# A long convolution with an MLP behind it: second DFT stage on half-height tiles, real and imaginary part on the two halves of the partitions, kv made channel-major

## The chip, the cores and the metric

One core of a Trainium2 chip. The time is the device time of one launch in microseconds (us). Engines are named as in the profile: PE is TensorE (PEld its weight loads), DVE is VectorE, ACT is ScalarE, POOL is GpSimd, SP is SyncE, which here only issues DMAs. PEclk is the TensorE clock that was granted, as a share of full speed.

## The reference

S = 2048 tokens, D = 512 channels, hidden width 1376, all inputs bf16. Part A is a gated long convolution, part B an MLP; both stand on a layer norm of what comes in, and both are added to it:

```python
def _A_ref(q, k, v, shift_k, ssm_k, ssm_D):          # q is layernorm(x)
    k_shift = zeros_like(k)                           # a causal filter of 4 taps per channel
    for t in range(ks):
        k_shift = k_shift + k_pad[:, t:t + S, :] * shift_k[:, ks - 1 - t][None, None, :]
    kv = k_shift * v
    kv_f = rfft(pad(kv, 2 * S)); kf_f = rfft(pad(ssm_k, 2 * S))     # per channel, over time, f32
    y = irfft(kv_f * kf_f)[:S] + kv * ssm_D[None, None, :]
    return q * y
h  = x + _A_ref(layernorm(x), k, v, shift_k, ssm_k, ssm_D)
h2 = h + relu(layernorm(h) @ w1) @ w2                # 512 -> 1376 -> 512
```

## The kernel before

The convolution is done per channel by a DFT of two stages with time split as t = 64 n1 + n2 (n1 below 32, n2 below 64) and frequency as 32 k1 by 64 k2. A channel is written d = 128 rg + 64 dp + g: rg picks one of four row groups, dp a half, g one of 64.

- **Loading (lines 155 to 248).** SP issues k and v in 4 KB rows per partition (`_load_p16`, 32 partitions per DMA; `kh`, `vt`), the filter `ssm_k` in one DMA (`sk`, 2 MB), and `ssm_D`, broadcast to `dtab_b`. PE transposes `sk` (L229), ACT copies the results into `kfl` (L230), whose partitions are (rg, n1). DFT tables are computed on chip: POOL makes indices, DVE phases (`_phase`), ACT sines (`_sin`, `_cos`). `cc`, `cs`, `cn` are [128, 32, 128] in float32r and block-diagonal: 64 x 64 blocks for dp = 0 and 1, zeros elsewhere.
- **Taps (L251 to L263).** DVE makes kv with tokens on the partitions: 8 chunks of 8 operations on 128 x 1024 elements. PE and ACT re-lay it into `xfl` (L277, L283).
- **Stage 1 (`_stage1`, L99 and L101), for the filter and then for kv:** 512 matmuls of 32 rows by 64 columns in four row groups, the table as a bf16 sum of two parts. 32 evacuations of 128 x 512 (all on ACT for the filter, L270; alternating ACT and DVE for kv, L302 and L304) write `a1k` or `a1x`: partitions (dp, n2), then 64 values (real and imaginary of each k1) by 256 channels (rg, g).
- **Stage 2 (`_stage2`, L112 to L115):** per k1 four full matmuls of 256 columns give the real and the imaginary part, [128, 2, 256] in PSUM, partitions (dp, k2). For the filter DVE and ACT store them into `kf` (L292 adds `ssm_D`, L294). For kv they are multiplied by `kf` straight from PSUM: DVE takes 3/4 of the columns (L334, L335: 128 x 384 each), POOL the last quarter (L336, L337) after ACT has copied it to SBUF (L333). Three k1 later `finish` adds the products up on PE (L344 to L347, identity and minus identity), and ACT writes the result over `kf` (L348).
- **Inverse, first stage (L388 to L396):** for each g two accumulating matmuls with `kf` as the stationary side (its elements 512 bytes apart) and 256 table columns moving; ACT and DVE copy into `bp`. In program order the layer-norm statistics of x (L382, L383) come before it; x itself (`xh`) is loaded behind the products.
- **Inverse, second stage, and MLP (L413 to L486):** `inv2_group` does 256 f32 matmuls in 32 x 32 tiles, reading `bp` at steps of 1 KB, then gate, residual, layer norm and transposes for four token tiles; `mlp1` and `mlp2` are bf16 matmuls with 512 columns; the groups are interleaved by hand.

The tile framework places the waits and moves independent instructions of an engine past each other by its own estimate; on the chip each engine then runs its list in order, and so does SP with its DMAs.

Of the kernel before, what the change touches and what calls it, by code (L numbers as in the profile page):

```python
# [8 lines left out]
ACT = mybir.ActivationFunctionType  # L9
# [9 lines left out]

# [33 lines left out]
def _phase(nc, pool, r_i32, col, F, M, name):  # L53
    t = pool.tile([P, F], I32, name=f"{name}_ti")
    nc.vector.tensor_scalar(out=t[:], in0=r_i32, scalar1=col[:], scalar2=float(M // 2), op0=ALU.mult, op1=ALU.add)
    nc.vector.tensor_single_scalar(out=t[:], in_=t[:], scalar=M - 1, op=ALU.bitwise_and)
    ph = pool.tile([P, F], F32, name=f"{name}_ph")
    nc.vector.tensor_single_scalar(out=ph[:], in_=t[:], scalar=-(M // 2), op=ALU.add)
    aph = pool.tile([P, F], F32, name=f"{name}_aph")
    nc.vector.tensor_scalar(out=aph[:], in0=t[:], scalar1=-1.0, scalar2=float(M // 2), op0=ALU.mult, op1=ALU.add)  # L60
    nc.vector.tensor_tensor(out=aph[:], in0=aph[:], in1=ph[:], op=ALU.max)
    return ph, aph


def _sin(nc, out, ph, M, neg=False):
    scale = 2.0 * math.pi / M * SIN_SHRINK
    nc.scalar.activation(out=out, in_=ph, func=ACT.Sin, scale=(-scale if neg else scale))


def _cos(nc, out, aph, M, halfpi):  # L70
    scale = 2.0 * math.pi / M * SIN_SHRINK
    nc.scalar.activation(out=out, in_=aph, func=ACT.Sin, scale=-scale, bias=halfpi[:])


def _load_p16(nc, dst, src2d, eng, halo=0, rows=None):
    S, D = src2d.shape
    r0, r1 = rows if rows is not None else (0, 16 + halo)
    for a in range(4):
        if halo and a == 0 and r0 < halo:
            ap = bass.AP(tensor=src2d.tensor, offset=src2d.offset, ap=[[64 * D, 32], [D, r1 - halo], [1, D]])  # L80
            eng.dma_start(out=dst[0:32, halo:r1, :], in_=ap)
            nc.vector.memset(dst[0:1, 0:halo, :], 0.0)
            ah = bass.AP(tensor=src2d.tensor, offset=src2d.offset + (64 - halo) * D, ap=[[64 * D, 31], [D, halo], [1, D]])
            eng.dma_start(out=dst[1:32, 0:halo, :], in_=ah)
        else:
            ap = bass.AP(tensor=src2d.tensor, offset=src2d.offset + (16 * a - halo + r0) * D,
                         ap=[[64 * D, 32], [D, r1 - r0], [1, D]])
            eng.dma_start(out=dst[32 * a:32 * a + 32, r0:r1, :], in_=ap)


def _stage1(nc, psum, src_fl, f1hi, f1lo, a_out, evac):
    cnt = 0
    for gb in range(8):
        pss = [psum.tile([P, 8, 64], F32, tag="ps", name=f"ps1_{rg}") for rg in range(4)]
        for gi in range(8):
            g = 8 * gb + gi
            for rg in range(4):
                rows = slice(32 * rg, 32 * rg + 32)
                nc.tensor.matmul(out=pss[rg][:, gi, :], lhsT=src_fl[rows, g, :, :], rhs=f1hi[rows, :],  # L99
                                 start=True, stop=False, tile_position=(32 * rg, 0))  # L100
                nc.tensor.matmul(out=pss[rg][:, gi, :], lhsT=src_fl[rows, g, :, :], rhs=f1lo[rows, :],  # L101
                                 start=False, stop=True, tile_position=(32 * rg, 0))
        for rg in range(4):
            j0 = 64 * rg + 8 * gb
            evac(cnt, a_out[:, :, j0:j0 + 8], pss[rg][:].rearrange("p g c -> p c g"))
            cnt += 1
# [411 lines left out]
```

## Time and profile before

| what | us |
|---|---|
| three runs | 291.29, 290.19, 288.76; median 290.19 |
| span of the profiled execution (first to last instruction) | 287.4 |
| mean granted PE clock in it | 0.85 |

The page gives no other time for that execution. By stage, from the busy times in windows (us busy in the window):

| window | stage | PE | DVE | ACT | POOL | PEclk |
|---|---|---|---|---|---|---|
| 0 to 43.7 | loading, tables, `kfl` | 9.8 | 38.4 | 24.2 | 16.3 | 0.83 |
| 43.7 to 59.5 | stage 1, filter | 12.7 | 15.8 | 15.7 | 0 | 0.50 |
| 59.5 to 64.1 | `xfl` | 3.3 | 3.8 | 4.6 | 0 | 0.50 |
| 64.1 to 82.3 | stage 2, filter | 18.2 | 13.5 | 15.1 | 0 | 0.85 |
| 82.3 to 96.3 | stage 1, kv | 8.2 | 10.1 | 8.6 | 0 | 0.66 |
| 96.3 to 131.9 | stage 2, kv, and products | 33.6 | 33.6 | 26.8 | 30.6 | 0.93 |
| 131.9 to 168.1 | inverse, first stage | 31.1 | 23.4 | 23.5 | 1.2 | 0.83 |
| 168.1 to 287.4 | inverse, second stage, MLP | 108.4 | 57.7 | 34.4 | 0 | 0.93 |

In the slices each digit is the busy share of 1/40 of the span in tenths (9 is 90% or more). In the groups a row is: line, engine, operation, out<-in, shape, count | busy us, mean ns of one | idle us of the engine just before, and what ended it. In the chain and the timeline a row is: start, length, what; in brackets the idle time before and who ended it.

### The profile page before, as it was taken

How to read it: one execution, taken by the hardware profiler on the slowest of the kernel's cores; microseconds unless marked ns; L12 is line 12 of the kernel's file. 1: busy time of each engine (PE TensorE's matmuls, PEld its weight loads, DVE VectorE, ACT ScalarE, POOL GpSimd, SP SyncE). 2: the span in 40 equal slices, each digit the busy share in tenths (PEclk: the TensorE clock that was granted, in tenths of full speed). 3: DMA queues.
4: the chain of work that ended last, by engine and by line, in shares of the span. 5: the costliest groups of instructions: out<-in, count | busy, mean ns of one | idle time of the engine just before them, and what ended most of it. 6: DMA issues, size and time to landing. Idle time of an engine off the chain costs nothing.

```text
span 287.4 us, 7594 instructions
## 1 busy us (share of the span) xinstructions
PE 225.3 (78%) x3098; PEld 156.9 (55%) x3108; DVE 196.2 (68%) x449; ACT 152.9 (53%) x327; POOL 48.0 (17%) x97
## 2 busy tenths in 40 slices
PE   2027007889986699988999385999999998999994
PEld 0027005529975699977999273544544554444441
DVE  4899999985896599996836936578294258233221
ACT  1039999998885278877966313464352045113000
POOL 9921000000000389983000000000000000000000
PEclk9999555556995599996899757589999999999999
DMA  5699400000000000029156000000000200020122
GB/s 120 150 344 229 98 0 6 5 2 0 2 3 5 2 2 2 2 66 208 22 183 211 0 2 5 2 2 1 5 0 5 57 18 0 18 57 0 38 56 55
DMA packets 7876, 14.25 MB, mean 50 GB/s; under 512 B 2210, under 2 KB 5634, under 8 KB 7714
## 3 DMA queue, kind: packets, MB, share of 16 engines
q1 hardware_dynamic: 4898, 11.31, 15.5%
q10 hardware_dynamic: 2944, 2.46, 3.0%
q8 instruction: 24, 0.39, 0.6%
q14 instruction: 10, 0.08, 0.1%
HBM read 11.67 MB, written 2.10 MB: 48 GB/s over the span
## 4 chain that ended last, share of the span: by engine, by line
PE 60%; ACT 11%; DVE 9%; issue 3%; DMA 2%; ACTq 0%; DVEq 0%; SPq 0%
PE ps2m L465 12%; PE ps1m L454 12%; PE pz L422 7%; ACT a1k L270 5%; PE psi L391 4%; PE psi L392 4%; DVE st L382 3%; PE ps L112 3%; PE ps L114 3%; PE ps L115 3%; PE ps L113 3%; PE pt L444 1%; DMA xh<-in_A_q_dram 1%; ACT xfl L283 1%; DVE a1x L304 1%
## 5 line engine op out<-in xcount | busy, mean ns | idle before, releaser
L454 PE MATMUL ps1m<-hlnT,w 128*128 128x512 bf16 (+1 forms) x169 | 41.6, 387 | 2.1 <-ACT h1T L457 1.0
L465 PE MATMUL ps2m<-w,h1T 128*128 128x512 bf16 (+1 forms) x173 | 38.4, 379 | 0.2
L468 DVE TENSOR_TENSOR o<-ps2m,xh 128x512 bf16<-128x512 f32 x16 | 11.1, 692 | 29.6 <-PE ps2m L465 17.8
L391 PE MATMUL psi<-dre,kf 128*128 128x256 f32 x64 | 26.4, 412 | 5.3 <-DVE bp L396 3.1
L454 PEld LDWEIGHTS <-w 128*128 128x128 bf16 (+1 forms) x176 | 17.0, 102 | 23.2 <-issue 7.8
L457 ACT ACTIVATE h1T<-ps1m 128x512 bf16<-128x512 f32 (+1 forms) x24 | 14.4, 599 | 27.4 <-PE ps1m L454 24.7
L465 PEld LDWEIGHTS <-h1T 128*128 128x128 bf16 (+1 forms) x176 | 17.2, 98 | 20.8
L422 PE MATMUL pz<-bp,ecore 32*32 32x128 f32 x1024 | 25.2, 393 | 3.5 <-ACT zt L428 2.1
L336 POOL TENSOR_TENSOR t<-usb,kf 128x128 fp32r<-128x128 f32 x32 | 15.1, 473 | 73.3 <-ACT usb L333 71.6
L392 PE MATMUL psi<-dim,kf 128*128 128x256 f32 x64 | 25.4, 397 | 0.0
L99 PE MATMUL ps<-f_hi,kfl 32*128 32x64 bf16 x256 | 10.3, 234 | 18.5 <-ACT kfl L230 15.7
L391 PEld LDWEIGHTS psi<-dre,kf 128*128 128x128 f32 x64 | 20.0, 313 | 7.1 <-DVE bp L396 3.4
L394 ACT COPY bp<-psi 128x256 f32<-128x256 f32 x48 | 17.8, 372 | 9.3 <-PE psi L392 7.6
L428 ACT CAST zt<-pz 128x512 bf16<-128x512 f32 x16 | 8.2, 600 | 26.4 <-PE pz L422 26.4
L348 ACT CAST kf<-psy 128x512 fp32r<-128x512 f32 x32 | 20.1, 631 | 3.6 <-POOL t L336 1.4
L422 PEld LDWEIGHTS pz<-bp,ecore 32*32 32x32 f32 x1024 | 15.5, 117 | 10.4 <-issue 4.1
L392 PEld LDWEIGHTS psi<-dim,kf 128*128 128x128 f32 x64 | 20.3, 317 | 0.0
L433 DVE TENSOR_TENSOR gt<-zt,qln 128x512 bf16<-128x512 bf16 x16 | 6.5, 407 | 19.8 <-ACT zt L428 19.8
L334 DVE TENSOR_TENSOR t<-ps,kf 128x384 fp32r<-128x384 f32 x32 | 17.6, 550 | 1.9 <-ACT usb L333 1.7
L459 DVE TENSOR_SCALAR h1T<-ps1m 128x512 bf16<-128x512 f32 x20 | 13.6, 682 | 7.1 <-PE ps1m L454 7.1
L229 PE MATMUL pst<-ident,sk 128*128 128x128 bf16 x64 | 6.7, 299 | 14.0 <-DMA sk<-in_A_ssm_k_dram 14.0
L335 DVE TENSOR_TENSOR t<-ps,kf 128x384 fp32r<-128x384 f32 x32 | 17.5, 548 | 0.0
(133 smaller groups left out, 575.7 us busy)
## 6 DMA issues: line engine op xcount, KB each, us to landing
vt<-in_A_v_dram SPq DMA_DIRECT2D x16, 128.0 KB, 8.4
sk<-in_A_ssm_k_dram SPq DMA_DIRECT2D x1, 2048.0 KB
xh<-in_A_q_dram SPq DMA_DIRECT2D x4, 512.0 KB, 8.4
kh<-in_A_k_dram SPq DMA_DIRECT2D x13, 128.0 KB, 4.5
w<-in_B_w_dram SPq DMA_DIRECT2D x1, 1376.0 KB, 6.4
w<-in_B_w_dram ACTq DMA_DIRECT2D x1, 1280.0 KB, 9.6
out_dram<-o SPq DMA_DIRECT2D x32, 32.0 KB, 1.5
out_dram<-o ACTq DMA_DIRECT2D x32, 32.0 KB, 1.7
```

The lines of the kernel that those rows point to most:

```text
L270: _stage1(nc, psum, kfl, f1hi, f1lo, a1k, lambda i, d, s: nc.scalar.copy(out=d, in_=s))
L334: nc.vector.tensor_tensor(out=t12v[:, :, 0:NV, :], in0=u[:, :, 0:NV, :], in1=k_same[:, :, 0:NV, :], op=ALU.mult)
L335: nc.vector.tensor_tensor(out=t34v[:, :, 0:NV, :], in0=u[:, :, 0:NV, :], in1=k_swap(0, NV), op=ALU.mult)
L336: nc.gpsimd.tensor_tensor(out=t12v[:, :, NV:DC, :], in0=usb[:], in1=k_same[:, :, NV:DC, :], op=ALU.mult)
L348: nc.scalar.copy(out=kf[:, :, k1, :, :].rearrange("p r g s -> p s r g"), in_=psy[:].rearrange("p s (r g) -> p s r g", r=DC))
L391: nc.tensor.matmul(out=pso, lhsT=kf[:, :, :, g, 0], rhs=dre[:], start=True, stop=False)
L392: nc.tensor.matmul(out=pso, lhsT=kf[:, :, :, g, 1], rhs=dim[:], start=False, stop=True)
L394: nc.scalar.copy(out=bp[:, g, :, :, :], in_=ps[:])
L422: nc.tensor.matmul(out=pz[32 * a:32 * a + 32, rg, l4, :], lhsT=ecore[rows, rho, n2, :], rhs=rhs, start=(rho == 0), stop=(rho == 1), tile_p ...
L454: nc.tensor.matmul(out=ps1[:fsz, :], lhsT=w1[:, c, fc * P:fc * P + fsz], rhs=hlnT[:, c, sc * SCW:(sc + 1) * SCW], start=(c == 0), stop=(c ...
L457: nc.scalar.activation(out=h1T[:fsz, fc, sc * SCW:(sc + 1) * SCW], in_=ps1[:fsz, :], func=ACT.Relu)
L465: nc.tensor.matmul(out=ps2[:], lhsT=h1T[:ksz, fc, t * P:(t + 1) * P], rhs=w2[:ksz, fc, :], start=(fc == 0), stop=(fc == NFC - 1))
```

## The change

Everything up to the second inverse stage is written anew; from there on only the layout of `bp` differs.

- **Filter:** `kfl` is loaded by 16 DMAs straight into its layout, in pieces of 128 bytes; the PE transposes of `sk` are gone. `ssm_D` enters in stage 1 as an impulse at time 0 (32 matmuls of 2 rows).
- **Taps:** k and v come channel-major, by transposing DMAs of 512 tokens (`kT`, two buffers; `vT`). The taps are four accumulating matmuls with diagonal weights per row group and chunk, interleaved with stage 2 of the filter; one DVE multiply by v per half chunk. 64 PE transposes make `xfl`.
- **Stage 1** has the same matmuls, and all evacuations alternate between ACT and DVE. Channels are ordered in pairs (a, rg, b) with g = 2a + b.
- **Stage 2** has no zero blocks: each dp half is its own tile of 64 rows by 128 columns, and the output has the real part on partitions 0 to 63 and the imaginary part on 64 to 127.
- **Products:** per k1 eight such matmuls give u and u with its halves swapped; DVE multiplies 44 of 64 pair columns (128 x 352 twice), POOL the other 20 (128 x 160 twice) after two ACT copies; two full matmuls of 512 columns (`m1`, `m2`) add up.
- **Order:** x is loaded and its statistics taken during the products; w1 and w2 are loaded behind them into the space of the stage 2 table.
- **Inverse, first stage:** one matmul of 128 rows and 128 columns per (dp, g), the stationary elements 8 bytes apart; evacuations of 128 x 1024 (10 on ACT, 6 on DVE). `bp` is laid out so that the second stage reads runs of 64.
- **Tables:** phases take two DVE operations instead of five.

```diff
-    sk = ld.tile([P, DC, S], BF16, name="sk")
-    nc.sync.dma_start(out=sk[:], in_=A_ssm_k.rearrange("(c p) t -> p c t", p=P))
+    kfl = flp.tile([P, 64, 2, 64], BF16, tag="fl", name="kfl")
+    for gh in range(2):
+        for rg in range(4):
+            for dp in range(2):
+                src = bass.AP(tensor=A_ssm_k.tensor, offset=A_ssm_k.offset + (128 * rg + 64 * dp + 32 * gh) * S,
+                              ap=[[64, 32], [S, 32], [1, 64]])
+                nc.sync.dma_start(out=kfl[32 * rg:32 * rg + 32, 32 * gh:32 * gh + 32, dp, :], in_=src)
...
+    for c in range(4):
+        kc = kvp.tile([P, DC, 528], BF16, tag="kT", name="kT", bufs=2)
...
+            nc.sync.dma_start_transpose(out=kc[:], in_=k_d[512 * c - 16:512 * c + 512, :])
+        nc.sync.dma_start_transpose(out=vT[:, :, 512 * c:512 * c + 512], in_=v_d[512 * c:512 * c + 512, :])
...
+    wt = wp.tile([P, 32, 4, 64], F32R, tag="w", name="wt")
...
+    def stage2(pss, k1, a_in, swapped):
+        for c in range(2):
+            blk = (2 - c) - (1 if swapped else 0)
+            for dp in range(2):
+                pq = slice(64 * dp, 64 * dp + 64)
+                nc.tensor.matmul(out=pss[dp], lhsT=wt[pq, k1, blk:blk + 2, :].rearrange("p b k -> p (b k)"),
+                                 rhs=a_in[pq, 32 * c + k1, :, :, :].rearrange("p a r b -> p (a r b)"),
+                                 start=(c == 0), stop=(c == 1), tile_position=(64 * dp, 0), skip_group_check=True)
...
+    def taps(c, half):
+        ps = psum.tile([P, 2, 512], F32, tag="ps", name="pkv")
+        for r in range(2):
+            rg = 2 * half + r
+            for j in range(KS):
+                nc.tensor.matmul(out=ps[:, r, :], lhsT=wdiag[:, rg, j, :], rhs=kT[c][:, rg, 16 - j:528 - j],
+                                 start=(j == 0), stop=(j == KS - 1))
+        vv = vT[:, 2 * half:2 * half + 2, 512 * c:512 * c + 512]
+        nc.vector.tensor_tensor(out=vv, in0=ps[:], in1=vv, op=ALU.mult)
+    for i in range(8):
+        spectrum_k(2 * i)
+        taps(i // 2, i % 2)
+        spectrum_k(2 * i + 1)
...
+    def product(k1):
...
+        u = psum.tile([P, 64, 2, DC, 2], F32, tag="u", name="u")
+        for s in range(2):
+            stage2([u[:, 32 * dp:32 * dp + 32, s, :, :].rearrange("p a r b -> p a (r b)") for dp in range(2)],
+                   k1, a1x, s == 1)
...
+        for s in range(2):
+            nc.scalar.copy(out=usb[:, s, :, :, kk, :], in_=u[:, NV:64, s, :, :])
+        for s in range(2):
+            nc.vector.tensor_tensor(out=t[:, s, 0:NV, :, :], in0=u[:, 0:NV, s, :, :], in1=kk_[:, 0:NV, :, :], op=ALU.mult)
+        for s in range(2):
+            nc.gpsimd.tensor_tensor(out=t[:, s, NV:64, :, :], in0=usb[:, s, :, :, kk, :], in1=kk_[:, NV:64, :, :], op=ALU.mult)
+    def finish(kp):
+        for kk, t in enumerate(pending.pop(0)):
+            psy = psum.tile([P, 512], F32, tag="psy", name="psy", bufs=4)
+            for s, m in ((0, m1), (1, m2)):
+                nc.tensor.matmul(out=psy[:], lhsT=m[:], rhs=t[:, s, :, :, :].rearrange("p a r b -> p (a r b)"),
+                                 start=(s == 0), stop=(s == 1))
+            nc.scalar.copy(out=kf_of(2 * kp + kk), in_=psy[:].rearrange("p (a r b) -> p a r b", r=DC, b=2))
...
-        nc.tensor.matmul(out=pso, lhsT=kf[:, :, :, g, 0], rhs=dre[:], start=True, stop=False)
-        nc.tensor.matmul(out=pso, lhsT=kf[:, :, :, g, 1], rhs=dim[:], start=False, stop=True)
+            y = kf[:, 32 * dp + (g0 + i) // 2, :, :, i % 2].rearrange("p r k -> p (r k)")
+            nc.tensor.matmul(out=ps[:, i, :], lhsT=y, rhs=dmat[:].rearrange("p a b -> p (a b)"), start=True, stop=True)
...
-                        rhs = bp[rows, :, rho, :, n2].rearrange("p g d -> p d g")
+                                         rhs=bp[rows, :, rho, n2, :],
```

## The prediction

> **What bounds the kernel now.** I read the page's slices first, then the chain of waits in order of time, then the groups kept apart by shape, then the timeline where two operations of one kind follow each other without a wait (a start-to-start pitch is what an engine can really do; a duration contains latency). The slices:
>
> ```profile
> PE   2027007889986699988999385999999998999994
> DVE  4899999985896599996836936578294258233221
> ACT  1039999998885278877966313464352045113000
> PEclk9999555556995599996899757589999999999999
> DMA  5699400000000000029156000000000200020122
> ```
>
> No engine is the bound throughout. Cut at the ends of its stages the span of 287.4 us is: loading, tables and re-layout to 43.7; first DFT stage of the filter to 59.5; re-layout of kv to 64.1; second stage of the filter to 82.3; first stage of kv to 96.3; second stage of kv with the products to 131.9; first inverse stage to 168.1; the rest to 287.4. In time order the chain says who ends each. From 43.77 it is ACT alone ("43.77 15.77 ACT a1k L270 x32"), then TensorE, and late in the inverse:
>
> ```profile
> 43.77 15.77 ACT a1k L270 x32
> 59.54 3.93 ACT xfl L283 x8
> ...
> 126.67 3.95 DMA xh<-in_A_q_dram
> ...
> 155.81 0.58 DVE st L382
> 156.47 0.57 DVE st L382
> ```
>
> and the timeline of TensorE shows what comes of the last of these:
>
> ```profile
> 165.39 0.58 PE L391 MATMUL psi<-dre,kf 128*128 128x256 f32 x1 [3.12 <-DVE bp L396]
> ```
>
> From 154.2 to 165 DVE runs the 16 layer-norm statistics, 0.66 us apart, while a PSUM tile waits for it behind them: about 10 us in which the inverse barely moves. The other two readings I use are a pair of weight loads and the DMA in two stretches (2.4 to 3.6 us, 128-byte packets of dtab_b; 21 to 30 us, 4 KB rows of k and v):
>
> ```profile
> L391 PEld LDWEIGHTS psi<-dre,kf 128*128 128x128 f32 x64 | 20.0, 313 | 7.1 <-DVE bp L396 3.4 <-ACT bp L394 2.7 <-ACT kf L348 1.0
> L114 PEld LDWEIGHTS ps<-a1k,c2c 128*128 128x128 f32 x32 | 6.9, 216 | 0.0
> ```
>
> ```profile
> DMA packets 470, 0.06 MB, mean 47 GB/s; under 512 B 470, under 2 KB 470, under 8 KB 470
> ...
> DMA packets 763, 2.09 MB, mean 232 GB/s; under 512 B 254, under 2 KB 254, under 8 KB 762
> ```
>
> **The change, stage by stage.** *Filter load.* L229's 64 transposes, L230's copies (the chain until 42.5) and sk go. kfl now comes by 16 DMAs in 128-byte pieces: 2048 x 512 x 2 B / 128 B = 16,384. The row for such pieces is dtab_b's: 470 packets in 1.2 us, 392 per us, so 41.8 us; by its 47 GB/s 44.6. I take 43, landing at 2.2 + 43 = 45.5. The other end is 232 GB/s (9 us), since the engines were only 29% busy in that stretch. The set-up work hides below: on DVE some 30 operations (8 of 1024 integers at about 0.9, twice L55's 0.48), on ACT eight sines of 1024 (1.2, twice L67's 0.63), on POOL four 512-element products (0.42 per 128 in L336's pitch, so 1.7 each): all done by about 25 us. If kfl came at 25, this cover would be gone. The first half of kfl lands by 24, so half of stage 1 runs early; after the last piece stay one row group's matmuls and eight evacuations over two engines (0.49 pitch on ACT, 0.60 on DVE): a1k ends at 50.5, against 59.5. The 32 matmuls that add ssm_D run before the wait.
>
> *Filter spectrum and taps, 50.5 on.* DVE's 8 x 7 tap operations on 1024 elements (0.60 pitch, 34 us beside ACT) and xfl's 64 regroupings go. In their place TensorE does 64 matmuls of 512 bf16 columns at L465's pitch 0.22: 14.1. Stage 2 takes 4 half-height matmuls per k1; if the two halves run side by side, as stage 1's four row groups do at 7 ns each in a burst, that is 64 x 0.1175 = 7.5 (0.1175 is the pitch of L112 to L115 at clock 1.0). Between half-height and full matmuls TensorE empties: a 256-column matmul lasts 0.28 and pitches 0.1175, so each of 16 changes costs about 0.16, 2.6 in all. Clock 0.5 for the first 3.4 us, as at 64 to 70 us now, adds 1.7, the last multiply 1.2: 27 us, end 77.5. DVE (16 x 0.60 + 8 x 1.2 = 19) and ACT (16 x 0.49) lie beside it. This holds if kT and vT are there. SP issues them behind kfl; a tap matmul waiting for kT holds all spectrum matmuls queued behind it, and kT of chunks 2 and 3 also wait for the taps of chunks 0 and 1. Four loads of k and four of v are 4.2 MB; the row nearest in source and size is the plain load of k and v at 232 GB/s: 18 us, 2.3 each. That is in time: chunk 3 is needed at 50.5 + 19 = 69.5. The trace has no transposing DMA, so the bounds are the 380 GB/s of 13 to 19 us, when sk landed (11 us), and, its rows being 256 B, the 392 small packets per us: 5.2 us each, 42 in all. The Trainium skill ("DMA: Bandwidth & Descriptors", Latency and other measured facts) gives a transposing DMA 261 GB/s with a non-contiguous middle dimension; by that the eight take an estimated 16 us, and nothing waits. No run here shows it.
>
> *Re-layout and kv's first stage.* 64 transposes at 0.105 (L229: 6.7 us) and the last 2048-element evacuation, twice L230's 1.03: 9 us, against 4.6. Stage 1 keeps its 512 matmuls and 32 evacuations: 14 as now. End: 45.5 + 5 + 27 + 9 + 14 = 100.5, **4.2 later** than 96.3.
>
> *Products.* Now TensorE (8 x 0.1175) and DVE (2 x 0.465 for 384 elements) are both at 0.94 per k1. Afterwards DVE has 2 x 352: 0.465 less 32/0.96 ns is 0.432 each, 27.6 for 64, plus the 16 statistics moved here, 10.5: 38.1. TensorE: 32 x (4 x 0.1175 + 2 x 0.22) = 29.1, plus 56 changes of height x 0.16 = 9: 38. ACT about 0.95 per k1 and POOL 2 x 0.42 x 160/128 = 1.05, 33.6, stay under. With fill and last pair 42, against 35.6: **+6.4**. xh is issued when xfl's transposes end and has the 14 us of stage 1 for its 10, so the statistics do not wait. How dear the changes are is open: six 32-row matmuls between full ones take 192.60 to 193.17, 0.57 us, where six of L422 in a run take 0.13. That is 0.44 a round trip instead of my 0.32, and by it the stage would be 3.5 us longer; without any drain TensorE would need 29.1 and DVE would set the stage alone. The Trainium skill ("TensorEngine Tiling (Array Packing)", Key Properties) has the rule behind that row, that changing the tiling mode drains TensorE, and it speaks against this change.
>
> *First inverse stage.* 128 matmuls as before, but of 128 columns, and the weights step 8 bytes instead of 512. L391's pitch is 0.22 at clock 0.5 (166.00 to 167.10) and at 1.0 alike: its 313 ns weight load sets it, not the clock. Bounds: 0.1175 (15.0 us) as with L114's dense weights, and 0.2235 (28.6). I take the first, since 8 bytes is nearer dense than 512. ACT: ten copies of 1024 (0.94 from pitches 0.27 at 256 and 0.49 at 512), eight sines at 0.6, a table load 1.3: 15.5; DVE 6.5 + 6.3. With the lead 17.5, against 36.2: **-18.7**; 10 of it are the statistics.
>
> *The rest* keeps its order; one Sqrt table load (1.3) comes back behind zt, **+0.7**. bp is read in runs of 64 instead of 1 KB steps; bounds 0 and -7 (L422 at 0.0218 against the 0.0133 that 4 x 128 columns over 16 tiles would take): I take 0. The w12 load has the whole inverse for its 10 us.
>
> **Sum.** 4.2 + 6.4 - 18.7 + 0.7 = -7.4: span 280.0. The page's execution gives no time but its span; the median of the runs lies 2.8 above it, which I add: **283**.
>
> **The rivals.** *Late transposes* (the other side): 256-byte rows at 392 per us, 42 us for the eight, so chunk 3 arrives at 89.5 instead of being wanted at 69.5: +20, **303**. It decides from 22 us for the eight on, 2.75 each. For: packets under 512 B ran at a fifth of the bandwidth. Against: k and v rows did not. *Strided weights stay slow*: 28.6 + 1 instead of 17.5, **295**. For: the same tensor is the stationary side in L391. *The halves do not run side by side*, so that the dense second stage saves nothing: 7.5 more in the spectrum, 15 in the products, **305**; against it stands stage 1's overlap of row groups. *A quick front*: kfl anywhere near 232 GB/s, bounded by the set-up at 25 us: stage 1 ends near 33, -18, **265**.
>
> **How the numbers follow.** Forecast 0.42 (275 to 292), late transposes 0.22, slow weights 0.15, serial halves 0.08, quick front 0.13. What a measurement here can tell from no change is about 1%, 287.3 to 293.1. Faster: 0.33 of the forecast and the quick front, 0.46. Same: 0.07 + 0.05 from the edges of the others, 0.12. Slower 0.42. The range 264 to 312 leaves out the faster half of the quick front and transposes slower than about 6 us each; the forecast's own range stands above.
>
> **What would show it.** kfl's last DMA near 45; no wait of pkv's matmuls for kT; the chain in TensorE from 50 to 85; DVE and TensorE both over 90% in the products; psi matmuls at 0.12 and the inverse under 20 us. I am wrong if PE idles on a DMA between 50 and 90, or if the pitch of psi is 0.22.

## The result, and the profile after

The changed kernel takes 302.97 us (median of four runs, 299.24 to 306.26) against 289.48 (287.27 to 291.29): the ratio is 1.042 with a 95% interval of 1.031 to 1.054. The ratio, like all ratios below, leaves out executions more than 1.5% above the fastest of their kernel, which keeps two of the four here and two of the ten of joint below. The forecast was 283 us, so the sign is wrong, though the time lies inside the range given (264 to 312); it lies outside the forecast's own (275 to 292). The profiled execution has a span of 297.5 us. Cut at the same places as the forecast:

| stage | forecast | measured | difference |
|---|---|---|---|
| filter in `a1k`, from 0 | 50.5 | 46.8 | -3.7 |
| filter spectrum and taps | 27.0 | 26.4 | -0.6 |
| `xfl` | 9.0 | 8.4 | -0.6 |
| stage 1, kv | 14.0 | 21.1 | +7.1 |
| products | 42.0 | 49.6 | +7.6 |
| first inverse stage | 17.5 | 29.5 | +12.0 |
| rest | 120.0 | 115.7 | -4.3 |
| span | 280.0 | 297.5 | +17.5 |

The slices come first again. PEclk is the row to look at: 0.5 from the twelfth to the fifteenth slice (82 to 112 us), again from about 160 to 186, and in parts up to 203.

```profile
PE   0406867998634599799986998499999998999994
PEclk9999999999955559999997555757999999999999
```

The chain of waits in order of time (start, length, what) shows the products late in their stage, two k1 in 134.07 to 136.72, all of it PE, and then what stands ahead of the inverse:

```profile
134.07 0.89 PE psy L351 x3
134.96 0.67 PE u L259 x8
135.63 0.43 PE psy L351
136.06 0.67 PE u L259 x8
...
153.08 0.62 POOL ec_r L383
...
156.31 1.33 ACT ecore L63 x2
157.64 0.91 ACT bp L412
158.55 0.04 issue
158.59 22.08 PE psi L406 x104
```

Two k1 take 2.66 us. The inverse stops at 156 until ACT has made a table and its first copy of `bp`, and then 104 matmuls take 22.08 us, 0.21 each, close to the 0.2235 of the kernel before; the forecast had put this pitch at 0.1175. The busy times of that line alone, in two windows (PE, PEld, then PEclk, DMA share, GB/s), show that it is not one pitch:

```profile
154.00:156.00 2.00, 2.00 (x18) 1.87 (x16) 1.00 1.03 400
...
164.00:168.00 4.00, 4.00 (x20) 3.90 (x20) 0.50 0.00 0
```

A window counts what reaches into it: eighteen matmuls at clock 1.0 in the first 2 us, in which PE also finishes the products, and twenty in 4 us at clock 0.5. From start to start the first 24 take 2.90 us, 0.12 each. The forecast's number holds there and for the first eight of the 104, until the clock falls at 159.6, and nowhere else.

The timeline of PE in stage 1 of kv holds the third surprise:

```profile
85.36 0.24 PE L246 MATMUL ps<-f_hi,xfl 32*128 32x64 bf16 x1
91.74 0.24 PE L246 MATMUL ps<-f_hi,xfl 32*128 32x64 bf16 x3 [6.15 <-issue]
```

For 6.15 us PE executes nothing, and no semaphore that the profile shows holds it. In the same microseconds `xh` is loaded (a window of PE: busy us, count, PEclk, DMA share, GB/s):

```profile
86.00:88.00 2.00, 0.00 (x0) 0.50 1.12 229
```

### The profile page after: what moved, and what is told of

It is laid out like the page before. It is cut to its first block, busy times and chain, and to the rows that moved or that the text cites. A ratio compares the mean times of both kernels' runs of the same rounds, so it can differ in the third digit from the quotient of the medians.

```text
span 297.5 us, 7556 instructions
## 1 busy us (share of the span) xinstructions
PE 236.9 (80%) x3186; PEld 151.8 (51%) x3200; DVE 172.3 (58%) x363; ACT 128.5 (43%) x255; POOL 54.0 (18%) x100
## 4 chain that ended last, share of the span: by engine, by line
PE 45%; DVE 11%; ACT 4%; DMA 3%; issue 1%; POOL 0%; DVEq 0%; ACTq 0%
PE ps1m L466 10%; PE ps2m L477 9%; PE psi L406 7%; PE u L259 7%; PE psy L351 7%; PE pz L433 5%; DMA out_dram<-o 3%; DVE st L447 2%; DVE o L480 1%; DVE t L343 1%; DVE gt L445 1%; DVE xh L446 1%; ACT h1T L469 1%; DVE hln L452 1%; PE pt L456 1%
## 5 line engine op out<-in xcount | busy, mean ns | idle before, releaser
L345 POOL TENSOR_TENSOR t<-usb,kf 128x160 fp32r<-128x160 f32 x64 | 37.5, 616 | 98.2 <-ACT usb L341 98.1
L343 DVE TENSOR_TENSOR t<-u,kf 128x352 fp32r<-128x352 f32 x64 | 30.4, 521 | 8.4 <-ACT usb L341 7.9
L406 PE MATMUL psi<-dmat,kf 128*128 128x128 f32 x128 | 25.1, 384 | 3.3 <-ACT bp L412 2.6
L239 PE MATMUL ps<-dmov,stat 2*128 2x512 bf16 x32 | 8.7, 595 | 23.7 <-DVE a1k L229 16.0
L351 PE MATMUL psy<-t,m 128*128 128x512 f32 x64 | 25.8, 476 | 2.2 <-DVE t L343 2.0
L259 PE MATMUL u<-a1x,wt 64*128 64x256 f32 x256 | 25.6, 324 | 2.3 <-DVE a1x L229 2.3
L406 PEld LDWEIGHTS psi<-dmat,kf 128*128 128x128 f32 x128 | 24.6, 296 | 3.9 <-ACT bp L412 2.7
L259 PEld LDWEIGHTS u<-a1x,wt 64*128 64x128 f32 x256 | 19.2, 206 | 11.7 <-ACT usb L341 5.5
L341 ACT COPY usb<-u 128x160 f32<-128x160 f32 x64 | 15.9, 306 | 13.0 <-PE u L259 12.6
L229 DVE CAST a1k<-ps 128x512 fp32r<-128x512 f32 x16 | 10.9, 691 | 15.8 <-ACT a1k L227 15.7
```

Of the source, the lines that this page charges most:

```text
L259: nc.tensor.matmul(out=pss[dp], lhsT=wt[pq, k1, blk:blk + 2, :].rearrange("p b k -> p (b k)"), rhs=a_in[pq, 32 * c + k1, :, :, :].rearrang ...
L341: nc.scalar.copy(out=usb[:, s, :, :, kk, :], in_=u[:, NV:64, s, :, :])
L343: nc.vector.tensor_tensor(out=t[:, s, 0:NV, :, :], in0=u[:, 0:NV, s, :, :], in1=kk_[:, 0:NV, :, :], op=ALU.mult)
L345: nc.gpsimd.tensor_tensor(out=t[:, s, NV:64, :, :], in0=usb[:, s, :, :, kk, :], in1=kk_[:, NV:64, :, :], op=ALU.mult)
L351: nc.tensor.matmul(out=psy[:], lhsT=m[:], rhs=t[:, s, :, :, :].rearrange("p a r b -> p (a r b)"), start=(s == 0), stop=(s == 1))
L406: nc.tensor.matmul(out=ps[:, i, :], lhsT=y, rhs=dmat[:].rearrange("p a b -> p (a b)"), start=True, stop=True)
```

## Experiments

Times of stages are of each kernel's profiled execution, read from the first and last instruction on the tiles. `a1k` is where the filter's first stage ends; the first inverse runs from the last psy matmul to the first pz matmul. Ratios are to the kernel before, measured beside it.

| kernel | a1k | products | first inverse | rest | span | runs: median, ratio |
|---|---|---|---|---|---|---|
| changed | 46.8 | 49.6 | 29.5 | 115.7 | 297.5 | 302.97, 1.042 |
| dense_weights | 46.8 | 62.5 | 29.9 | 116.0 | 312.4 | 320.08 |
| half_columns | 46.8 | 59.2 | 27.8 | 116.1 | 306.0 | 307.73 (one) |
| wide_columns | 46.8 | 49.8 | 23.6 | 115.3 | 291.5 | 293.58, 1.020 |
| no_mode_change | 48.5 | 52.9 | 29.8 | 116.5 | 303.9 | 305.65 (one) |
| stats_after | 48.4 | 47.2 | 30.7 | 114.5 | 296.3 | 297.93, 1.036 |
| late_xh | 46.8 | 46.9 | 28.2 | 117.1 | 288.3 | 290.07 (one) |
| bp_steps | 46.8 | 58.5 | 29.8 | 118.7 | 310.9 | 312.64 (one) |
| two_queues | 44.5 | 52.2 | 29.9 | 116.3 | 298.9 | 298.88, 1.026 |
| eight_slices | 40.4 | 59.7 | 29.9 | 115.2 | 306.3 | 301.88, 1.035 |
| joint | 40.6 | 65.3 | 24.2 | 115.1 | 299.9 | 289.49, 0.989 |
| joint_late_stats | 40.3 | 47.0 | 29.8 | 114.6 | 287.3 | 288.71, 0.998 |
| early_stats | 44.2 | 48.6 | 23.7 | 115.6 | 282.4 | 283.44, 0.980 |
| early_stats_slices | 46.1 | 48.6 | 23.6 | 113.7 | 281.7 | 283.71, 0.985 |

### What sets the pitch of the first inverse stage

The rival in the forecast blamed the 8-byte step of the weights. A second suspect was the short moving side.

**dense_weights**

```diff
-    kf = slotB.tile([P, 64, DC, 32, 2], F32R, tag="B", name="kf")
+    kf = slotB.tile([P, 64, 2, DC, 32], F32R, tag="B", name="kf")
-        return kf[:, :, :, k1, :]
+        return kf[:, :, :, :, k1].rearrange("p a b r -> p a r b")
-            y = kf[:, 32 * dp + (g0 + i) // 2, :, :, i % 2].rearrange("p r k -> p (r k)")
+            y = kf[:, 32 * dp + (g0 + i) // 2, i % 2, :, :].rearrange("p r k -> p (r k)")
```

> kf is laid out as [half-frequency, pair, row group, k1] in place of [half-frequency, row group, k1, pair], so that the 128 weights of each first-inverse matmul lie side by side (4-byte step in place of 8); the moving side stays 128 columns. Theory S (the step of the weights sets the pitch of 0.21 us): pitch 0.06 to 0.12, the 128 matmuls in 15 us, the stage then limited by ACT's copies and sines, 18 to 21 us from the end of the last psy copy in place of 29; the run 8 to 11 us under the changed kernel, 292 to 295. Theory C (128 fp32r columns cost 0.21 whatever the weights are): pitch and time as in the changed kernel, 303. In both cases the products write and read kf with a 128-byte step; if DVE or ACT minds, the products' stage grows from 49.6 and its rows show it.

**half_columns**

```diff
-            nc.tensor.matmul(out=ps[:, i, :], lhsT=y, rhs=dmat[:].rearrange("p a b -> p (a b)"), start=True, stop=True)
+            nc.tensor.matmul(out=ps[:, i, 0:64], lhsT=y, rhs=dmat[:, 0, :], start=True, stop=True)
```

> The first inverse stage streams only the 64 real-part columns against each weight block (the imaginary half of bp gets a copy of the real one, so that half of the transform is left out); weights, counts and copies stay. Theory S: the pitch stays at 0.21 us, the stage at 29 us. Theory C: the pitch halves to about 0.11 and the stage falls to about 20 us.

Both suspects fall. In dense_weights 128 matmuls take 27.66 us, 0.216 each, all of them at granted clock 0.5; in half_columns 26.02, 0.203 each: the first fifteen are 0.12 apart and at clock 1.0, the rest 0.213. The groups of dense_weights in 100 to 196 us (busy us, mean ns) show that the layout has a price of its own:

```profile
L343 DVE TENSOR_TENSOR t<-u,kf 128x352 fp32r<-128x352 f32 x64 | 49.4, 837 | 2.8 <-ACT usb L341 2.2
L345 POOL TENSOR_TENSOR t<-usb,kf 128x160 fp32r<-128x160 f32 x64 | 44.8, 725 | 104.5 <-ACT usb L341 104.0
L353 ACT CAST kf<-psy 128x512 fp32r<-128x512 f32 x32 | 36.7, 1163 | 3.1 <-PE psy L351 2.9
...
L406 PEld LDWEIGHTS psi<-dmat,kf 128*128 128x128 f32 x128 | 27.5, 332 | 1.4 <-ACT kf L353 1.4
```

With `kf` touched in 128-byte steps the DVE multiply takes 837 ns (521 in the changed kernel), ACT's write 1163 (627), POOL's 725 (616), and the products 62.5 us.

The remaining reading: a weight load of 128 fp32r columns takes 0.12 us at clock 1.0 and 0.21 at 0.5, and a matmul that streams 128 columns fills only half of it, so that the clock does not come back. Then more streaming should make the stage shorter.

**wide_columns**

```diff
-            nc.tensor.matmul(out=ps[:, i, :], lhsT=y, rhs=dmat[:].rearrange("p a b -> p (a b)"), start=True, stop=True)
+            nc.tensor.matmul(out=ps[:, i, :, :], lhsT=y,
+                             rhs=dmat[:].rearrange("p a b -> p (a b)").unsqueeze(1).to_broadcast([P, 2, P]), start=True, stop=True)
...
-        srcv = ps[:].rearrange("p g f -> p f g")
+        srcv = ps[:, :, 0, :].rearrange("p g f -> p f g")
```

> Each weight block of the first inverse stage streams the 128 columns of dmat twice (256 columns, the second half is written to PSUM and not read); two PSUM tiles of four banks in place of three of two; results as before. The step of the weights and the number of columns are both excluded as cause of the pitch by now: 0.216 us with dense weights, 0.20 with 64 columns, 0.12 in the first 24 of the changed kernel, at granted clock 1.0. Theory G (a 128x128 fp32r weight load takes 0.11 us at clock 1.0 and twice that at 0.5, and a stream that fills only half of the loads' time does not bring the clock back to 1.0): with the array streaming all the time the clock returns to 1.0 some 6 us after the stage starts, as in the kernel before at 137.9, the pitch goes from 0.22 to 0.12 and the 128 take 6 + 101 x 0.12 = 18 us in place of 27; the stage 20 to 23 us in place of 29 and the run 6 to 9 us under the changed kernel, 294 to 297, though twice as many columns are streamed. Rival H (the clock stays at 0.5 for a fixed time after the pause of 2.7 us ahead of it, whatever is streamed): pitch 0.22 to the end, 303 or slightly more.

Streaming each column twice takes 9.4 us off the median of the runs and 6.0 off the span. The weight loads of wide_columns late in the stage (timeline; start, length):

```profile
168.03 2.03 PEld L406 LDWEIGHTS psi<-dmat,kf 128*128 128x128 f32 x16 [0.52 <-ACT bp L413]
```

Sixteen in 2.03 us, less the last one's own length of 0.2: 0.122 us from start to start. The clock is 1.0 in every window from 150 to 184; it never fell. So this run alone does not decide between theory G, by which streaming brings the clock back about 6 us into the stage, and rival H, by which the clock stays at 0.5 for a fixed time after a pause of about 2.7 us, whatever is streamed: PE's pauses here are eight of 0.20 to 0.90 us, 3.65 in all (2.4 for ACT, 1.2 for DVE), none as long as the 2.58 of the changed kernel. joint, further down, does more, for it has the same 256 columns and its clock did fall in this stage, at 161.8 (windows of PE: busy us, count, PEclk, DMA share, GB/s):

```profile
160.00:164.00 4.00, 3.32 (x16) 0.72 1.02 391
164.00:168.00 4.00, 3.43 (x22) 0.86 0.88 282
168.00:172.00 4.00, 3.09 (x24) 1.00 0.00 0
```

The matmuls go from 0.12 to 0.213 apart, and at 165.2 the clock is whole again. joint_late_stats is a second case: after a pause of 3.90 us PE resumes at 155.73 with clock 0.5 and has 1.0 at 159.7. With 64 or 128 columns the clock fell in this stage in nine profiles, and in none did it come back before the stage ended, 20 us or more later. So H falls and G's observation holds: with 256 columns the clock returns. Why the columns matter no run shows, nor whether the PSUM tiles, two of four banks in place of three of two, play a part. Nor is a long pause needed for the fall: in late_xh the clock fell at 145.8, 2 us into the stage, with a pause of 0.68 us ahead of it and none above 0.4 since 100.

With the clock up the stage still takes 23.6 us: what ends it now is the chain of tables and copies, ACT, DVE and POOL in turn. Of the +12.0 the clock explains 5.9; the other 6 are that chain, which the forecast had put at 17.5 by adding up ACT alone.

### What sets the products

**no_mode_change**

```diff
-            stage2([u[:, 32 * dp:32 * dp + 32, s, :, :].rearrange("p a r b -> p a (r b)") for dp in range(2)],
-                   k1, a1x, s == 1)
+            for dp in range(2):
+                for c in range(2):
+                    blk = (2 - c) - s
+                    nc.tensor.matmul(out=u[:, 32 * dp:32 * dp + 32, s, :, :].rearrange("p a r b -> p a (r b)"),
+                                     lhsT=wt[:, k1, blk:blk + 2, :].rearrange("p b k -> p (b k)"),
+                                     rhs=a1x[:, 32 * c + k1, :, :, :].rearrange("p a r b -> p (a r b)"),
+                                     start=(c == 0), stop=(c == 1))
```

> In the products the eight half-height matmuls of a k1 become eight full-height ones of the same 256 columns (the output is not the convolution: both halves are summed), so that nothing changes height any more. Pure streaming is then 8 x 0.1175 = 0.94 per k1, where four pairs side by side would take 0.47. Theory M (halves run side by side, and each change of height costs about 0.2 us): eight take 0.94 in place of 0.66 us, psy's two 0.43 without the 0.9 seen for three, a period of 0.94 + 0.44 = 1.38 per k1 against 1.33 now: no gain, about 1.5 us longer in the stage. Theory N (the halves never ran side by side and 0.66 is what eight cost): 0.66 stays and the period stays 1.33.

Its chain of waits, two k1 from 145.26 to 148.22:

```profile
145.26 0.23 PE psy L356
145.50 0.95 PE u L333 x8
146.46 0.69 PE psy L356 x3
147.15 1.07 PE u L333 x8
```

Theory M holds. Eight full-height matmuls need 0.95 to 1.07 us where eight half-height ones need 0.67 with their change, so the halves do run side by side. And without a change of height one psy matmul takes 0.23 in place of 0.43 and three 0.69 in place of 0.89: a change costs 0.20 us. Two k1 of the changed kernel are then 8 x 0.1175 + 4 x 0.22 + 4 x 0.20 = 2.62, measured 2.66. The period without changes was 1.48 per k1, a little above the 1.38 expected.

**stats_after**

```diff
-    st1 = late.tile([P, NT, 6], F32, name="st1")
...
     ecp = pl.push("ecp", side="right")
+    st1 = ecp.tile([P, NT, 6], F32, name="st1")
```

> The 16 layer-norm statistics write to tiles whose space comes free only after the products, so that they run in the first inverse stage; xh is still loaded at 80 us. Theory B (their bunch on DVE makes the multiplies late and costs the 6.3 us in which TensorE stands, 119.9 to 126.2, though DVE has time for them over the whole stage): the products' stage falls from 49.6 to 42 to 44 us (32 x 1.33 and the ends), and the inverse, whose matmuls need 28 us at 0.215, takes the statistics with a loss of 0 to 4 us; run 297 to 301. Rival (POOL, 2.34 of 2.66 us per two k1, or TensorE sets the stage and the stall is made up later): stage 47 or more.

The products fall to 47.2 us, not to 42 to 44. The stop of 6.3 us is gone, but it had cost only 2.4 net; the stage is 32 x 1.33 = 42.6 and the rest is mostly the clock, which is 0.5 until 114 in it and until 112 in the changed kernel. The statistics in the inverse cost it 1.2 us. What the stop does otherwise is seen in bp_steps below and in the spread of the runs: 297.0 to 298.1 here, 299 to 306 with the stop (though joint_late_stats, without the stop too, spreads from 285 to 301).

### The load of xh beside kv's first stage

**late_xh**

```diff
-    late = pl.push("late", side="right")
-    xh = late.tile([P, NT, D], BF16, name="xh")
-    _load_tokens(nc, xh, x_d, nc.sync)
...
     pl.pop("prod")
+    late = pl.push("late", side="right")
+    xh = late.tile([P, NT, D], BF16, name="xh")
+    _load_tokens(nc, xh, x_d, nc.sync)
```

> The load of xh and the statistics go behind the products. Theory F (TensorE's stop of 6.15 us from 85.6 to 91.7 in kv's first DFT stage, with no semaphore behind it, is its instructions not coming in while the four loads of xh, 2 MB, keep the 16 DMA engines at 1.0): no such stop, kv's first stage takes 14 to 15 us in place of 21, and the products start at 96 to 97. Rival (the stop belongs to the code itself, as with a jump): it stays. In the inverse the statistics stand behind the last copy of bp in DVE's order and wait for xh, so up to 10 us come back there; the run 293 to 301.

Theory F holds. The same window of late_xh:

```profile
86.00:88.00 2.00, 1.47 (x96) 0.50 0.03 8
```

PE goes on, and kv's first stage takes 14.6 us (81.5 to 96.1) in place of 21.1: the 14 of the forecast. That what fails to come is PE's own instructions is an inference: PE was held by no semaphore, and the stop goes with the load. It is not the load alone: early_stats loads the same 2 MB from 93 to 102 us, beside the products, and PE shows no such stop there. The stage executes some 100 instructions of each kind in 2 us, more than any other but the second inverse, where the same thing is seen below.

### Where the rest gained

**bp_steps**

```diff
-    bp = slotA.tile([P, 2, 2, 64, 64], F32, tag="A", name="bp")
+    bp = slotA.tile([P, 64, 2, 2, 64], F32, tag="A", name="bp")
```

> bp is stored as the kernel before stored it, [half-frequency column g, dp, rho, n2], so that the second inverse stage reads its 128 columns in steps of 1 KB again. If the 3.6 us that the changed kernel gains behind the first inverse stage (115.7 in place of 119.3) come from the contiguous rows, the 1024 small matmuls take 25 us in place of 21 and the rest 119 to 120; if from somewhere else (clock, order), 115 to 116. The copies to bp no longer transpose: their mean of 1.0 (ACT) and 1.2 us (DVE) may change, which the inverse, bound by its matmuls, doesn't show.

The group of small matmuls, in bp_steps from 191.5 on:

```profile
L433 PE MATMUL pz<-bp,ecore 32*32 32x128 f32 x1024 | 25.2, 394 | 3.8 <-ACT zt L440 2.2 <-DVE qln L442 1.1 <-issue 0.5
```

and in the changed kernel:

```profile
L433 PE MATMUL pz<-bp,ecore 32*32 32x128 f32 x1024 | 21.2, 337 | 3.5 <-ACT zt L440 2.3 <-DVE qln L442 1.1
```

With 1 KB steps the 1024 matmuls are back at 25.2 us, the kernel before's figure, and the rest at 118.7: 3.0 of the 4.3 us that the rest came in under the forecast are the contiguous rows. The products, which the edit doesn't touch, took 58.5 us. There DVE's bunch of statistics stopped PE until 129.3, the clock fell to 0.5 at 131.3 and stayed there until 148.2. half_columns and eight_slices have 59.2 and 59.7 in another way: without such a fall, their clock was at 0.5 from the start of the products until about 141 and 140.

### The front

**two_queues**

```diff
-                nc.sync.dma_start(out=kfl[32 * rg:32 * rg + 32, 32 * gh:32 * gh + 32, dp, :], in_=src)
+                (nc.sync if rg < 2 else nc.scalar).dma_start(out=kfl[32 * rg:32 * rg + 32, 32 * gh:32 * gh + 32, dp, :], in_=src)
```

> Row groups 2 and 3 of kfl are issued from ACT's queue in place of SP's; by this the planned order of TensorE in the filter's first stage becomes all four row groups in turn, where it was one pair of row groups after the other. Theory O (the stage lasts 37 us from the first matmul at 10.2 to 46.8 because of that order: TensorE stands behind evacuations of one pair while the other is wanted): a1k ends at 30 to 36, the span falls by 10 to 16 us. Theory L (the landing of kfl in 128-byte pieces sets it): a1k ends where it did, within 3 us, unless the two queues land sooner. Theory E (16 + 16 evacuations and what stands before them on ACT and DVE set it): a1k ends at about 22.5 + 16 x 0.85 = 36 at the earliest, so 36 to 42.

**eight_slices**

```diff
-    for gh in range(2):
+    for gh in range(8):
...
-              ap=[[64, 32], [S, 32], [1, 64]])
+              ap=[[64, 32], [S, 8], [1, 64]])
```

> kfl comes in 64 loads of 8 half-columns each in place of 16 loads of 32, on SP's queue alone, in the same 128-byte pieces; the planned order of TensorE in the filter's first stage is then all four row groups in turn. Theory O (its 24 us from the first evacuation at 22.5 to 46.8 come from the order by row-group pairs; with the regular order two_queues needed 14.1 from its first evacuation at 30.3 to 44.5): a1k ends at 36.6 to 39, the span falls by 8 to 10 us, 288 to 290, the run 291 to 295. Rival I (what 64 issues cost on SP, at 0.35 to 0.8 us each 22 to 51 us, holds the last pieces and the transposing loads behind them): a1k ends at 46 or later and pkv's matmuls wait for kT; no gain or a loss.

In the changed kernel the DMAs of `kfl` and the evacuations of stage 1 stand so (count, ns shortest/median/longest, first and last start):

```profile
L114 SPq DMA_DIRECT2D kfl<-in_A_ssm_k_dram x16: 312/796/987, 0.7 to 13.5; - x16
...
DMA to landing us min/median/max: 2.5/3.8/4.2
```

```profile
L227 ACT CAST a1k<-ps x16: 562/588/609, 22.5 to 45.4; 128x512 fp32r<-128x512 f32 x16
```

and the evacuations of two_queues:

```profile
L227 ACT CAST a1k<-ps x16: 562/592/619, 30.3 to 43.0; 128x512 fp32r<-128x512 f32 x16
```

`kfl` has landed by 13.5 + 4.2 = 17.7 us. Then 24.3 us go from the first evacuation to the end at 46.8, because the planned order on PE runs one pair of row groups after the other and PE stands behind evacuations; with all four in turn the same 32 evacuations and matmuls take 14.2 (30.3 to 44.5). Theory O is right on the cause, and theory E falls: in the changed kernel ACT and DVE do nothing but these evacuations from 22 to 47, and still take 24 us for them. But the gain is used up: eight issues on ACT's queue keep its first sine from starting until 18.8 (9.1 in the changed kernel), and only 2.3 us remain at `a1k`. In eight_slices 64 issues keep SP busy until 35.7; `a1k` ends at 40.4, and then PE waits 3.0 us for the transposing loads of k, 2.75 of them at 58, after which the clock is at 0.5 until 62: the rival of the forecast come true in another kernel. Spectrum and taps take 31.5 us, and 5 of the 6.4 us are lost.

### Putting the repairs together

**joint** (eight slices, 256 columns, and the places of `flp` and `kvp` exchanged)

```diff
-    kvp = pl.push("kvp", side="right")
     flp = pl.push("flp", side="right")
+    kvp = pl.push("kvp", side="right")
```

> Three of the repairs at once, results as before: kfl in eight slices, xh loaded when the last matmul of kv's first stage has read xfl (their places in SBUF are exchanged), so that it comes during the products, and 256 columns in the first inverse stage. If the causes are independent the span is 297.5 - 9 (order) - 6 (xh beside the first stage) - 6 (clock in the inverse) = 276 to 278, the run 278 to 283, under the kernel before by 2 to 4 per cent. Rival (xh beside the products holds TensorE's instructions there, or the statistics wait for xh and so stop the multiplies): the products' stage over 50 us and the run 284 to 290.

**joint_late_stats** (joint, and `st1`, `mv1`, `rstd1` as in stats_after)

> As joint, and the statistics run behind the products, where they write to space that comes free then. The products then have no stop (47 us as in stats_after, and no danger that the clock falls after it); the inverse, which with 256 columns is bound by copies and tables on ACT and DVE (23.6 us in wide_columns), takes 12 us of statistics on DVE: 25 to 30. Run 279 to 286; under joint only if the stop in the products costs more than the 2 to 6 us that the inverse then loses.

The pieces worked: in joint kv's first stage takes 14.7 us and the inverse 24.2. The sum didn't come: runs go from 283.1 to 301.7, and their median of 289.49 lies above the 288.12 of the kernel before beside it. In the profiled execution the products take 65.3 us, at half clock for 46 of them (windows of PE):

```profile
100.00:108.00 8.00, 8.00 (x34) 0.50 0.46 94
...
132.00:140.00 8.00, 8.00 (x34) 0.50 0.01 2
140.00:148.00 8.00, 8.00 (x58) 0.92 0.01 2
```

The statistics can't be the reason: the chain meets none before 149. joint_late_stats has 47.0 in the products, but the statistics and 256 columns together bring the inverse back to 29.8.

**early_stats** (256 columns, exchanged places, and the statistics from an own copy of x in the filter's first stage)

```diff
+    xs = setup.tile([P, NT, D], BF16, name="xs")
+    _load_tokens(nc, xs, x_d, nc.scalar)
...
     stage1(kfl, a1k, True)
+    ln1_stats(range(0, 16))
```

> As wide_columns, with xh loaded behind kv's first stage (as in joint, no slices of kfl), and with the 16 statistics done from a copy of x of their own, loaded at the start from ACT's queue, on DVE in the filter's first stage, where DVE is busy 10.9 of 23 us. Theory D (the bunch of statistics is what stops TensorE and lets the clock fall in the products): products 47 us with the clock at 1.0 from their 9th us on in every run, inverse 23 to 24, and no wide spread: front 47 to 50, products from 96 to 99 on, span 281 to 286, run 283 to 288. Theory P (the products' matmuls with their changes of height don't hold the clock by themselves): products of 55 us or more in some runs, and a spread of over 10 us as joint had.

**early_stats_slices** (the same with `kfl` in 32 loads)

> As early_stats, with kfl in 32 loads of 16 half-columns (order of TensorE in part regular; 64 loads held the transposing loads up, 32 need about 18 us on SP's queue). If the front is what joint lost to waits for kT, a1k ends at 42 to 45 and nothing waits for kT: 2 to 5 us under early_stats, 279 to 285; if the statistics on DVE set the front now, as early_stats.

early_stats has a lower median than either: 283.44 us, against 288.32 for the kernel before beside it, ratio 0.980 with an interval of 0.975 to 0.984. It has no stop in the products and the inverse of wide_columns. But two of its six runs took 293.7 and 297.0, so theory D is not enough. The clock granted on average over a whole run was 0.925 to 0.933 in the four short runs and 0.887 and 0.870 in these two; neither was profiled, so no run shows in which stage they lost it. In its profiled execution the clock came back 13 us after the products began at 94.5:

```profile
104.00:108.00 4.00, 4.00 (x21) 0.60 0.02 4
108.00:112.00 4.00, 4.00 (x31) 1.00 0.00 0
```

against 9 in the changed kernel and 46 in joint, with nothing but PE on the chain in all three after the first 2 to 3 us. In the thirteen profiles whose products change height the clock came back 8.5 to 46 us after their start; in the two without changes of height it took 3.3 us (no_mode_change) and about 4 (the kernel before, 96.3 to 100.4). That fits theory P, that the products as they are don't reliably bring the clock back, but these are single executions of each kernel. What decides in which execution it comes back soon was not found. The slices gained nothing here, `a1k` ended later (46.1).

### The stall in the kernel before

**before_act_copies**

```diff
-        if g % 4 != 3:
-            nc.scalar.copy(out=bp[:, g, :, :, :], in_=ps[:])
-        else:
-            nc.vector.tensor_copy(out=bp[:, g, :, :, :], in_=ps[:])
+        nc.scalar.copy(out=bp[:, g, :, :, :], in_=ps[:])
```

> The kernel before, with one edit: all 64 copies of bp go to ACT, where every fourth went to DVE. If the reading of the profile before is right, that the inverse barely moves for 10 us since a PSUM tile waits on DVE behind the 16 statistics, TensorE then goes on at its pitch of 0.2235 (128 matmuls, 28.6 us) and ACT needs 64 x 0.27 to 0.37 and eight sines at 0.6, 22 to 29 us: the first inverse stage falls from 36.2 to 30 or 31, the run by 5 to 6 us to 283. The statistics then end at 165 and the second inverse stage is not held. Rival (ACT's 64 copies and the sines set the stage, or the second stage then waits for the statistics): 34 us or more, no gain.

The second inverse starts at 163.7 in place of 168.1, so the stage fell by 4.4 us, less than the 5 to 6 expected and than the 10 that I read off the profile. The timeline of PE in the kernel before has the reason. Beside the pause of 3.12 us that the forecast showed, it has three like this one, at 159.12, 160.30 and 161.47:

```profile
159.12 0.49 PE L391 MATMUL psi<-dre,kf 128*128 128x256 f32 x1 [0.46 <-ACT bp L394]
```

That is 4.5 us in all, and until 158 PE had kept its pitch. The run did not gain: 290.37 us, ratio 1.008 (1.005 to 1.011). The timeline of PE in before_act_copies:

```profile
163.71 3.84 PE L419 MATMUL pz<-bp,ecore 32*32 32x128 f32 x183 [0.46 <-ACT bp L393]
170.90 1.98 PE L419 MATMUL pz<-bp,ecore 32*32 32x128 f32 x73 [3.35 <-issue]
```

The small matmuls now meet the load of w2, issued at 163.4 and moving up to 407 GB/s, and PE stops for 3.35 us without a semaphore, as beside `xh`. Then the square root of the statistics stands on ACT behind three copies `zt` until 174.5, and the first `qln` starts at 176.5.

## Why the prediction was wrong

**The step that failed is the pitch of the first inverse stage.** I took 0.1175 us for it, the pitch of the dense matmuls in the filter's second stage, and had no term for the clock. That row has two pitches in the same trace: 0.2135 from start to start while the clock is at 0.5, 0.1175 at 1.0 (windows of the kernel before: PE, PEld, DVE, ACT and POOL busy, then PEclk, DMA share, GB/s):

```profile
66.00:68.00 2.00, 2.00 (x11) 2.00 (x11) 0.96 (x3) 2.00 (x6) 0.00 (x0) 0.50 0.00 0
...
70.00:72.00 2.00, 2.00 (x20) 2.00 (x19) 1.69 (x5) 1.56 (x4) 0.00 (x0) 1.00 0.00 0
```

The new stage does the same, 0.12 at 1.0 and 0.21 at 0.5, and after 159.6 its clock was 0.5. From L391's 0.22 at both clocks I concluded that the weight load sets the pitch and not the clock. For weights in 512-byte steps that may be so, and no run tests it; for the new shape it was not. And the change itself took away what brings the clock back in this stage: with 256 columns per weight load it returned within about 4 us (joint, joint_late_stats), with 128 not in 20. The rival "strided weights stay slow" gave the right 29 us and the wrong cause: dense weights change nothing.

**The chain of tables and copies** was the second half of that term: 17.5 was ACT's busy time plus a lead, where ACT, DVE and POOL hand the tables on in turn and need 23.6.

**The products** (42 forecast, 49.6). I named two prices for a change of height and took the lower, 0.16; the six 32-row matmuls between full ones said 0.22, and 0.20 was measured. That is 64 changes x 0.20 = 12.8 where I had counted 56 at 0.16, 9: +3.8 of the 7.6. The stop by the bunched statistics is 2.4; I had checked DVE's sum over the stage (38.1), not when the statistics come. That leaves 1.4. The clock in the first 9 us, where two sets of eight and their psy take 1.15 and 0.72 in place of 0.66 and 0.43 and two k1 4.60 (107.10 to 111.70) in place of 2.66, cost more than that, an estimated 2.7 for some 6.5 us at that pace; my allowance for the fill must have taken up the difference. The Trainium skill ("TensorEngine Tiling (Array Packing)", Key Properties), which I quoted for the drain, gives the rule and no price.

**Stage 1 of kv** (14, 21.1): "has the 14 us of stage 1 for its 10" was said of `xh` as if it cost PE nothing there. It cost 6.2 to 6.5.

**The front** came out 3.7 us better by two errors that cancel. Pieces of 128 bytes landed at 16,384 in 17 us, about 960 per us, not at dtab_b's 392; 470 packets at the very start of the run were no measure of the rate. And stage 1 took 24 us from its first evacuation where I had nearly all of it hidden under the load. So the "quick front" rival was right on the transfer and wrong on what follows.

**Right:** spectrum and taps (27, 26.4) and `xfl`; that the halves run side by side; that the transposing loads are in time (4.6 us to landing each, nothing waits for them), though by less margin than I had: eight_slices moved them back by 20 us and they were late. The contiguous rows of `bp`, which I took at 0 within 0 to -7, gave -3.0.

**Ten us of statistics** in the old inverse were misread. While DVE ran them PE kept its pitch until 158, and its pauses add up to 4.5 us, of which before_act_copies gives back 4.4. The 17.5 does not rest on the ten, for it was added up anew. The run gained nothing from the shorter stage, since what comes next was not ready sooner.

The Trainium skill ("TensorE: Matmul & The Clock Gate", Part 1) says that the clock halves after an idle window of about 3.4 us and is whole again after one busy window of that length. The kernel before fits it loosely: PE resumed at 131.9 and had the full clock at 137.9. The changed kernel does not, if busy is what the profile calls busy: PE was busy in every microsecond from 159 to 180, and from 159.6 the clock stayed at 0.5; in the products of joint it did so for 46 us. Nor did every fall follow an idle window of that length: in late_xh the longest pause ahead of it was 0.68 us.

## What to carry to other kernels

Before pricing a TensorE stage by a pitch, read the granted clock beside the row, and see in a run whether the new shape lets the clock come back: here 64 columns per weight load in place of 128 saved next to nothing, and 256 took 6 us off the stage. Look at what moves beside a burst of many small matmuls: a load that costs no semaphore can still stop TensorE. And check an engine that is shared for when its work comes, not only for its sum.

## What the runs showed of the hardware

- Matmuls that each have their own load of 128 x 128 fp32r weights follow one another every 0.12 us with the clock at 1.0 and every 0.21 at 0.5, with 64, 128 or 256 columns alike (half_columns, changed kernel, joint). Weights in steps of 8 or 4 bytes made no difference (changed kernel, dense_weights); those in 512-byte steps had 0.2235 at both clocks (kernel before).
- Such loads with 128-column matmuls back to back for 22 us left the clock at 0.5; with 256 columns it was back at 1.0 within about 4 us (joint, joint_late_stats).
- A change between half-height and full-height matmuls cost 0.20 us (no_mode_change).
- Two big loads, 2 MB of x at 160 to 250 GB/s and w2 at up to 407, went with stops of PE of 6.15 and 3.35 us with no semaphore, both while PE executed its smallest matmuls.
- Elements 128 bytes apart cost DVE 837 in place of 521 ns for 352 fp32r elements, and ACT 1163 in place of 627 ns for 512.
- 128-byte pieces land at some 960 per us over 16 DMAs; an issue of 1024 of them takes 0.80 us on SP and 1.5 on ACT's queue beside it.
